# Spacing of the spectrum units, the gate of the second filter group, and one table copy in a Fourier mixing and MLP kernel

## The chip, the cores and the metric

The kernel runs on one core of one Trainium2 chip. The metric is the device time of one execution in microseconds. A core has a matrix engine (TensorE, PE in the profile; PEld is its weight load), a vector engine (VectorE, DVE), a scalar engine (ScalarE, ACT), a general engine (GpSimd, POOL) and a queue engine (SyncE, SP). DMAs are issued from SP, ACT and POOL, and 16 DMA engines carry them. Matrix results land in PSUM and are evicted from there by VectorE or ScalarE.

## The reference

```python
def _attn_ref(x, filt_r, filt_i):            # x: (8, 3008, 256)
    X = np.fft.rfft(x, axis=1)
    Y = X * (filt_r + 1j * filt_i)[None, :, :]
    return np.fft.irfft(Y, n=x.shape[1], axis=1).astype(np.float32)

def _moe_ref(x, w_in, w_out, beta):          # d_model 256, d_ff 2048
    h = x @ w_in
    g = h * (1.0 / (1.0 + np.exp(-beta * h)))
    return (g @ w_out).astype(np.float32)

out = _moe_ref(_attn_ref(x, filt_r, filt_i).reshape(24064, 256), w_in, w_out, beta)
```

Eight images of 3008 positions and 256 channels are each filtered in the frequency domain along the positions, and all 24064 rows then go through a two-layer network with a Swish whose slope is per hidden unit.

## The kernel before

**The transform.** 3008 is 47 times 64. The kernel computes the real Fourier transform by matmuls with small tables: a first stage over 47 points, with data `x` and table `t1` (`s1`, L610, line L616), a second over 64 points with `t2` (`s23`, L631, line L638), then the product with the filter, the inverse over 64 points with `t3` (line L664), and the inverse over 47 points with `t4` (`s4`, L679, its matmuls in `last4`, L541). Between the stages the data is turned through DRAM scratch: `a1` is written as `d` (L621) and read back as `a2` (L628), `z` is written as `d` (L669) and read back as `zz` (L676). All these DMAs are on SP's queue, in the order of the program, and each waits there for what it needs; the stores of the result (`store`, L784) share that queue.

**The main loop** (L812) has 47 blocks of 512 rows, each of 16 steps, 752 in all. A step has two matmuls of 128x512 into `hps` (L825), an activation by ScalarE into `gT` (L834), and, two steps later, four matmuls of 128x256 into the accumulators `acc` (L867). At the end of a block VectorE and ScalarE evict `acc` to `ost`. The transform of image b+1 is laid between these steps: `place` (L693) spreads a list of units over a range of steps, `plan` holds for each step the units in the order in which they were placed, and they are issued after the step's `hps` matmuls and before its `acc` matmuls. A first placed unit goes to the start of the range, the following ones to evenly spaced steps rounded down; with `clear` a unit is moved off the first two and last two steps of a block; a step takes at most `per` units.

**A spectrum unit** (`s23`, 15 per image) covers two of the 24 frequencies. Unit i issues two matmuls L638 into a PSUM tile `ps2`, three VectorE operations that read it and the filter (`p_t` L649, `q_t` L650 and L653), an addition `v_t` on GpSimd (L654), and, for the v of three units earlier (VLAG), two matmuls L664 into a PSUM tile `ps3`, which ScalarE evicts to `z` (L667, in the profile as L107). Units 0 to 2 have only the first half, units 12 to 14 only the second. After every third `z` the group is written as `d`. `ps2` and `ps3`, and the PSUM tiles of `s1`, `s4`, `turn_z` and `last_z`, come from one pool, `fpsum`, tag "f", of 3 buffers.

**The start** (up to L591) treats image 0 apart and through no DRAM. GpSimd issues six DMAs of `x` (X_FIRST, L124), the third of which holds j = 8 to 15 and the fifth j = 16 to 23 of 80 partitions, then the first of four groups of the filter `fri`. The other three groups (12 DMAs) are on SP behind a small DMA `mark` (L198), which reads a row of `x` and so waits for the chunk that holds it. VectorE computes angles for the first half of the table `t2`, GpSimd for the second (`angles`, L260); ScalarE turns them into sines and cosines (`t2_part`), and `t2_more` (L287) completes a half by three operations: the negated cosines, a copy of the sines (slot 2 to 3) and a copy of the cosines (slot 1 to 0). The `held` copies (L407) on GpSimd wait for the filter's third group and stand before the loads of `win_sb`, `w_out` and the first half of image 1 on GpSimd's queue. Then a loop of 14 rounds (L490 on) has `product(i)`, two VectorE multiplications by the filter (L444), transposes, tables and `inverse3` (L461).

Of the kernel before, what the change touches and what calls it, by code (L numbers as in the profile page):

```python
# [9 lines left out]
P = 128  # L10
# [3 lines left out]
F32 = mybir.dt.float32  # L14
# [10 lines left out]
M = 64  # L25
H = M // 2
NK = 24
J = 32
KG = 6
NG = NK // KG  # L30
JG = 8
# [6 lines left out]
def kernel(  # L38
# [10 lines left out]
    nc = tc.nc  # L49

    B, S, D = x.shape
# [35 lines left out]
    fri = consts.tile([P, NK, D], F32, name="fri", tag="fri")  # L87
# [6 lines left out]
    t2 = consts.tile([P, NK, 5, M], BF16, name="t2", tag="t2")  # L94
# [18 lines left out]
    def load_x(b, parts, t=None):  # L113
        if t is None:
            t = xpool.tile([NP, J, D], BF16, name="xg", tag="xg")
        xv = x[b].rearrange("(p j) d -> p j d", j=J)
        for p0, p1, j0, j1 in parts:
            nc.gpsimd.dma_start(t[p0:p1, j0:j1, :], xv[p0:p1, j0:j1, :])  # L118
        return t
# [3 lines left out]
    X_HALVES = [(0, 80, 0, J // 2), (80, NP, 0, J // 2), (0, 80, J // 2, J), (80, NP, J // 2, J)]  # L123
# [16 lines left out]
    def staged(i):  # L140
        return frr[:, NK - NFB + i * WG : NK - NFB + (i + 1) * WG, :]

    def load_wout(i):
        nc.gpsimd.dma_start(
            staged(i),
            moe_w_out[i * WG * P : (i + 1) * WG * P, :].rearrange("(fb fp) j -> fp fb j", fp=P),
        )
# [12 lines left out]
    setup = sp.enter_context(tc.tile_pool(name="setup", bufs=1))  # L160
# [32 lines left out]
    x_cur = load_x(0, X_FIRST)  # L193
# [1 line left out]
    nc.sync.dma_start(bt[:], moe_beta.rearrange("(fb fp) -> fb fp", fp=P))  # L195

    mark = dpool.tile([1, D], BF16, name="mark", tag="mark")
    nc.sync.dma_start(mark[:], x_cur[:1, JG, :])  # L198

    gp = nc.gpsimd  # L200
    ip_f = small("ip_f")
# [55 lines left out]
    NH = NK // 2  # L257
# [16 lines left out]
    def t2_part(h, part):  # L274
        u, r = us[h], rs[h]
        ks_ = slice(h * NH, (h + 1) * NH)
        if part == 0:
            nc.scalar.activation(t2[:, ks_, 2, :], u[:], ACT.Sin, scale=TWO_PI)
        elif part == 1:
            nc.scalar.activation(r[:], u[:], ACT.Abs)  # L280
        else:
            for cols, sgn, b in ((slice(0, H), -1.0, hp), (slice(H, M), 1.0, hm)):
                nc.scalar.activation(
                    t2[:, ks_, 1, cols], r[:, :, cols], ACT.Sin, scale=sgn * TWO_PI, bias=b[:]
                )

    def t2_more(h, eng):  # L287
        ks_ = slice(h * NH, (h + 1) * NH)
        nc.vector.tensor_scalar_mul(t2[:, ks_, 4, :], t2[:, ks_, 1, :], -1.0)
        eng.tensor_copy(t2[:, ks_, 3, :], t2[:, ks_, 2, :])  # L290
        eng.tensor_copy(t2[:, ks_, 0, :], t2[:, ks_, 1, :])


    m_p = small("m_p")
# [23 lines left out]
    def first1(i, on_act):  # L318
        for dc in range(NDC):
            if dc:  # L320
                ps = opsum.tile([P, 4, P], F32, name="psa", tag="acc")
            else:
                ps = fpsum.tile([P, 4, P], F32, name="psa", tag="f")
            for e in range(4):
                nc.tensor.matmul(  # L325
                    ps[:, e, :KP],
                    lhsT=x_cur[:, 4 * i + e, dc * P : (dc + 1) * P],
                    rhs=t1b[:],
                    start=True,
                    stop=True,  # L330
                )
            evac(
                a_t[:, dc, :, 4 * i : 4 * i + 4, :].rearrange("p k j a -> p j k a"),
                ps[:, :, :KP].rearrange("p j (k a) -> p j k a", a=4),
                on_act[dc],
            )
# [33 lines left out]
    first1(3, (False, False))  # L370
    warm(2)

    t2_more(0, nc.vector)
    first1(4, (False, False))
    warm(2)
    first1(5, (True, True))
# [24 lines left out]
                )  # L401
        evac(a2s[-1][:, 3 * (i % 2) : 3 * (i % 2) + 3, :], pb[:], on_act)


    held = setup.tile([P, 1], F32, name="held", tag="held")
    for p0 in (H, M + H):
        gp.tensor_copy(held[p0 : p0 + H], fri[p0 : p0 + H, 3 * KG - 1, :1])  # L407
    def load_win(h):
        fs = slice(h * FF // 2, (h + 1) * FF // 2)
        gp.dma_start(win_sb[:, :, fs], moe_w_in[:, fs].rearrange("(dc p) f -> p dc f", p=P))  # L410

    load_win(0)
    load_win(1)
    load_wout(0)
    xs = {}
    if B > 1:
        xs[1] = load_x(1, X_HALVES[:2])
    turn_a(0, False)
    turn_a(1, True)

# [59 lines left out]
    def table4():  # L480
        for src, dst in ((t1b, t4b), (t1, t4)):
            tp = opsum.tile([KP, NP], BF16, name="tp", tag="acc")
            nc.tensor.transpose(tp[:], src[:], ident[:NP, :NP])
            nc.scalar.activation(dst[:], tp[:], ACT.Copy)
# [4 lines left out]
    for i in range(NK // 2 + FLAG):  # L489
        if 0 < i < NK // 2:  # L490
            product(i)
        if i % 3 < 2 and i // 3 < 3:
            turn_a(2 + 2 * (i // 3) + i % 3, True)
        if i < 3:
            t2_part(1, i)
        if i in TAB:
            n = TAB.index(i)
            table3(1 + n // 2, 2 - 2 * (n % 2), n % 2 == 0 or n == 5)()
        if i == 3:
            t2_more(1, nc.vector)  # L500
            for h in range(1, 4):
                load_wout(h)
            if B > 1:
                load_x(1, X_HALVES[2:], xs[1])
                mark3 = dpool.tile([1, D], BF16, name="mark3", tag="mark3")
                nc.sync.dma_start(mark3[:], xs[1][:1, J - 1, :])
        if i == 11:
            table4()

            bps = hpsum.tile([P, NFB], F32, name="bps", tag="hps")  # L510
            nc.tensor.transpose(bps[:], bt[:], id_f[:])
            nc.scalar.activation(beta_sb[:], bps[:], ACT.Copy)
        if i == NK // 2:
            nc.vector.reciprocal(rbeta_sb[:], beta_sb[:])
        if i >= FLAG:
            inverse3(i - FLAG)
# [106 lines left out]
    def a2_read(b):  # L623
        s = st[b]
        s["a2"] = []
        for h in range(NG):
            t = a2pool.tile([P, KG, D], BF16, name="a2", tag="a2")
            nc.sync.dma_start(t[:], s["d1c"][:, h * KG : (h + 1) * KG, :])  # L628
            s["a2"].append(t)
# [60 lines left out]

    plan = {}

    def place(a, z, units, clear=False, per=1):  # L693
        last_at = a
        for n, go in enumerate(units):
            at = a + (z - a) * n / max(1, len(units) - 1)
            at = max(int(at), last_at)
            if clear and (at % NFB < 2 or at % NFB > 13):
                at += (2 - at) % NFB
            while len(plan.get(at, ())) >= per:  # L700
                at += 1
            plan.setdefault(at, []).append(go)
            last_at = at
        return last_at

    def u1(b, act=False):
        def unit(i):
            def go():
                if i == 0:
                    start(b)  # L710
                s1(b, i, act and i % 2 == 1)

            return go

        return [unit(i) for i in range(J // 2)]

    def u23(b):
        return [lambda i=i: s23(b, i) for i in range(NK // 2 + VLAG)]
# [4 lines left out]
    def uz(g, act=False):  # L723
        return [lambda i=i: turn_z(g, i) for i in range(2)] + [
            lambda i=i: last_z(g, i, act) for i in range(2 * NDC)
        ]
# [26 lines left out]
    units = uz(3, True)  # L753
# [4 lines left out]
    if B > 1:  # L758
        units = u1(1, True)
        place(3, 8, units[: J // 4], per=2)  # L760
        place(10, 10, uf(0, JG), per=9)
        at = place(9, 14, units[J // 4 :], per=9)
        place(at + 1, at + 1, [lambda: a2_read(1)] + uf(JG, NK), per=9)
        place(14, 20, ut(4), per=2)
        at = place(25, 56, u23(1), per=2)
        assert at < 60
        place(60, 60, [lambda: zz_read(1)], per=9)
        place(67, 79, u4(1), per=2)
    if B > 2:
        place(36, 36, ux(2), per=9)  # L770
        at = place(50, 66, u1(2, True), per=3)
        assert at < 74
        place(74, 74, [lambda: a2_read(2)], per=9)
    for b in range(2, B):
        a = first_step[b - 1]
        place(a + 3, a + 47, u23(b), True)
        place(a + 53, a + 53, [lambda b=b: zz_read(b)], per=9)
        if b + 1 < B:
            place(a + 6 if b == 2 else a - 8, NBLK * NFB, ux(b + 1), per=9)
            place(a + 48, a + 61, u1(b + 1))  # L780
            place(a + 68, a + 68, [lambda b=b: a2_read(b + 1)], per=9)
        place(a + 63, a + 78, u4(b))
# [29 lines left out]
    for s in range(len(steps) + LAG):  # L812
        if s < len(steps):
            i, fb = steps[s]
# [4 lines left out]
            while pos < t0 + tn:  # L819
                b, n0 = divmod(pos, S)  # L820
# [20 lines left out]
        if s >= LAG:  # L841
            i, fb = steps[s - LAG]
# [15 lines left out]
            per = acc[0].shape[1]  # L858
# [16 lines left out]
            if fb == NFB - 1:  # L875
                for h, a in enumerate(acc):
# [5 lines left out]
                    eng = nc.scalar if last and h >= 2 else nc.sync  # L882
# [31 lines left out]
```

## Time and profile before

| | us |
|---|---|
| median of 3 runs | 785.22 (784.85 to 785.43) |
| profiled execution | 785.37 |
| its span on the core | 783.3 |
| PE busy | 768.8 (98%) |
| PEld busy | 547.8 (70%) |
| ACT busy | 594.4 (76%) |
| DVE busy | 393.3 (50%) |
| POOL busy | 144.4 (18%) |
| HBM | 57.16 MB read, 46.66 MB written |

The granted TensorE clock is 1.0 throughout. Times in the profile count from the start of the span. In a timeline row the first number is the start, the second the duration, then engine, line, operation, output and inputs, and what the engine waited for just before. Matmuls are pipelined and their ends are modelled, so the distance between the starts of two matmuls says more than the idle time between them. Where a helper evicts PSUM, the line is the helper's (L107 for ScalarE, L109 and L111 for VectorE). A few matmul records are missing from the trace and leave a hole of the matmul's own length.

### The profile page before, as it was taken

What the parts mean: (1) busy time and instruction counts of PE and PEld (TensorE: products, weight loads), DVE (VectorE), ACT (ScalarE), POOL (GpSimd) and SP (SyncE); (2) the same over time, 40 slices, a digit from 0 to 9 for tenths busy, and PEclk for the clock granted to TensorE, in tenths of its full rate; (3) what the DMA queues carried; (4) which work ended last, traced back from release to release, by engine and by line L of the source; (5) the groups of instructions that cost most, each with busy time, mean ns of one, the idle gap of its engine ahead of it and who ended that gap; (6) DMA issues with size and microseconds to landing.
All of it is one profiled execution on the core that took longest, in us unless ns stands there. A gap on an engine that the chain in (4) does not pass through costs nothing.

```text
span 783.3 us, 15454 instructions
## 1 busy us (share of the span) xinstructions
PE 768.8 (98%) x6015; PEld 547.8 (70%) x6111; DVE 393.3 (50%) x645; ACT 594.4 (76%) x922; POOL 144.4 (18%) x143
## 2 busy tenths in 40 slices
PE   8899999999999999999999999999999999999997
PEld 5767667666776667866668666786667766776665
DVE  7848836646446563474635746267452761500101
ACT  6987887886678867787677876778767788677776
POOL 8522501320013100231002310024000330000000
PEclk9999999999999999999999999999999999999999
DMA  9979764517801186022850238412371114100101
GB/s 190 253 174 228 176 191 132 128 67 202 221 28 68 68 209 194 28 81 94 197 167 28 95 111 183 149 64 81 108 209 40 64 68 128 49 34 28 55 28 54
DMA packets 84185, 91.46 MB, mean 117 GB/s; under 512 B 4498, under 2 KB 74276, under 8 KB 83154
## 3 DMA queue, kind: packets, MB, share of 16 engines
q1 hardware_dynamic: 81008, 73.95, 30.8%
q0 software_dynamic: 2816, 16.26, 10.7%
q8 instruction: 48, 0.79, 0.4%
q10 hardware_dynamic: 288, 0.26, 0.1%
q14 instruction: 25, 0.20, 0.1%
HBM read 57.16 MB, written 46.66 MB: 133 GB/s over the span
## 4 chain that ended last, share of the span: by engine, by line
PE 96%; ACT 1%; issue 1%; DMA 1%; DVE 1%; POOL 0%; DVEq 0%; POOLq 0%
PE acc L867 43%; PE hps L825 39%; PE ps L616 3%; PE ps L541 3%; PE ps L664 3%; PE ps L638 2%; DMA xg<-in_x_dram 1%; PE psz L461 1%; PE pz L533 0%; PE psa L325 0%; ACT a L107 0%; DVE q_t L653 0%; DVE q_t L650 0%; PE pt L351 0%; PE ps L435 0%
## 5 line engine op out<-in xcount | busy, mean ns | idle before, releaser
L834 ACT ACTIVATE gT<-hps,beta_sb 128x512 bf16<-128x512 f32 x752 | 515.6, 687 | 176.5 <-PE hps L825 155.4
L867 PE MATMUL acc<-wout_sb,gT 128*128 128x256 bf16 x3008 | 451.4, 272 | 2.7
L825 PE MATMUL hps<-y,win_sb 128*128 128x512 bf16 (+8 forms) x1636 | 427.6, 350 | 0.4 <-ACT gT L834 0.3
L867 PEld LDWEIGHTS <-gT 128*128 128x128 bf16 x3008 | 285.6, 98 | 127.6 <-ACT gT L834 0.2
L825 PEld LDWEIGHTS <-win_sb 128*128 128x128 bf16 x1730 | 165.0, 98 | 24.7 <-issue 0.6
L654 POOL TENSOR_TENSOR v_t<-p_t,q_t 128x512 bf16<-128x512 f32 x84 | 106.6, 1269 | 390.4 <-DVE q_t L653 327.6
L109 DVE COPY ost<-acc 128x512 f32<-128x512 f32 (+1 forms) x88 | 56.2, 677 | 192.6 <-PE acc L867 189.6
L109 DVE CAST a<-ps 96x512 bf16<-96x512 f32 x96 | 65.9, 686 | 87.3 <-PE ps L616 86.8
L111 DVE TENSOR_SCALAR y<-ps 128x376 bf16<-128x376 f32 (+1 forms) x119 | 63.9, 544 | 61.3 <-PE ps L541 61.2
L649 DVE TENSOR_TENSOR p_t<-ps,frr 128x512 f32<-128x512 f32 x84 | 58.1, 692 | 31.3 <-PE ps L638 28.9
L653 DVE TENSOR_TENSOR q_t<-ps,fri 64x512 f32<-64x512 f32 x84 | 58.2, 693 | 1.2
L650 DVE SCALAR_TENSOR_TENSOR q_t<-ps,fri 64x512 f32<-64x512 f32 x84 | 57.4, 684 | 1.1
L541 PEld LDWEIGHTS <-zz 96*128 96x128 bf16 x512 | 35.3, 97 | 29.3 <-issue 0.5
L107 ACT ACTIVATE z<-ps 128x512 bf16<-128x512 f32 x84 | 49.5, 589 | 0.0
L616 PE MATMUL ps<-xg,t 94*96 94x512 bf16 x112 | 42.1, 381 | 0.7
L541 PE MATMUL ps<-t,zz 96*128 96x94 bf16 x448 | 36.7, 205 | 1.1
L664 PE MATMUL ps<-v_t,t 128*128 128x256 bf16 x168 | 32.2, 274 | 0.8 <-DVE q_t L653 0.3
L638 PE MATMUL ps<-a,t 128*128 128x256 bf16 x168 | 32.1, 273 | 0.4
L118 POOL DMA_DIRECT2D xg<-in_x_dram x22 | 12.1, 552 | 101.7 <-PE acc L867 97.6
L638 PEld LDWEIGHTS <-t 128*128 128x128 bf16 x168 | 15.8, 98 | 14.6
L664 PEld LDWEIGHTS <-t 128*128 128x128 bf16 x168 | 15.3, 98 | 10.8 <-ACT z L107 3.8
L616 PEld LDWEIGHTS <-t 94*96 94x96 bf16 x112 | 13.6, 123 | 11.8
(120 smaller groups left out, 195.0 us busy)
## 6 DMA issues: line engine op xcount, KB each, us to landing
out_dram<-ost SPq DMA_DIRECT2D x80, 256.0 KB, 2.1
d<-a SPq DMA_DIRECT2D x28, 384.0 KB, 3.4
a<-d SPq DMA_DIRECT2D x28, 384.0 KB, 4.4
d<-z SPq DMA_DIRECT2D x28, 384.0 KB, 2.3
zz<-d SPq DMA_DIRECT2D x28, 384.0 KB, 6.8
xg<-in_x_dram POOLq DMA_DIRECT2D x6, 1280.0 KB, 10.0
frr<-in_filt_r_dram SPq DMA_DIRECT2D x12, 256.0 KB, 7.5
out_dram<-ost SPq DMA_DIRECT2D x18, 128.0 KB, 2.5
```

What stands on the lines that cost most here:

```text
L109: nc.vector.tensor_copy(dst, src)
L111: nc.vector.tensor_scalar_mul(dst, src, scale)
L541: nc.tensor.matmul(ps[:, e, :NP], lhsT=zz[:, jj + e, dc * P : (dc + 1) * P], rhs=tab[:], start=True, stop=True,)
L616: nc.tensor.matmul(ps[:KP], lhsT=t1[:], rhs=s["x"][:, 2 * i : 2 * i + 2, :], start=True, stop=True)
L638: nc.tensor.matmul(ps[:, e, :], lhsT=t2[:, k0 + e, 3:5, :].rearrange("p c k -> p (c k)"), rhs=s["a2"][g][:, kk + e, :], start=True, stop=True,
L649: nc.vector.tensor_tensor(p_t[:], ps[:], frr[:, ks_, :], ALU.mult)
L653: nc.vector.tensor_tensor(q_t[:M], ps[M:P], fri[M:P, ks_, :], ALU.mult)
L654: nc.gpsimd.tensor_tensor(v_t[:], p_t[:], q_t[:], ALU.add)
L664: nc.tensor.matmul(ps[:, e, :], lhsT=t3[:, k0 + e, :], rhs=v_t[:, e, :], start=True, stop=True)
L825: nc.tensor.matmul(hps[:, pos - t0 : pos - t0 + ln], lhsT=win_sb[:, dc, fb * P : (fb + 1) * P], rhs=ys[b][:, dc, n0 : n0 + ln], start=(dc ...
L834: nc.scalar.activation(gT[:, :tn], hps[:, :tn], ACT.Silu, scale=beta_sb[:, fb : fb + 1])
L867: nc.tensor.matmul(acc[tb // per][:, tb % per, :], lhsT=g_[:, tb * P : (tb + 1) * P], rhs=wout_sb[:, f_, :], start=(f_ == 0 and tb % per = ...
```

## The change

1. `place` gets a parameter `gap`, the least distance in steps between consecutive units of a list. The spectrum units use 2: those of image 1 (also spread over 25 to 58 in place of 25 to 56) and those of images 2 to 7.
2. The first transform of image 2 goes to steps 54 to 68 instead of 50 to 66, and its `a2_read` to 75 instead of 74.
3. `mark` reads row j = 16 of `x` instead of j = 8, so the SP loads of filter groups 2 to 4 start behind the fifth DMA of `x` (the third chunk along j) instead of the third DMA.
4. The copy of the sines becomes `t2_sin`. For the first half it stays on VectorE; for the second it is on GpSimd, in round 0 of the loop, behind its angles. `t2_more` keeps the other two operations.
5. The `held` copies and the loads behind them become `late_loads`, called in round 0 after that copy. On GpSimd's queue their order among themselves is unchanged.

```diff
-    nc.sync.dma_start(mark[:], x_cur[:1, JG, :])
+    nc.sync.dma_start(mark[:], x_cur[:1, 2 * JG, :])
...
-    def t2_more(h, eng):
+    def t2_sin(h, eng):
+        ks_ = slice(h * NH, (h + 1) * NH)
+        eng.tensor_copy(t2[:, ks_, 3, :], t2[:, ks_, 2, :])
+
+    def t2_more(h):
         ks_ = slice(h * NH, (h + 1) * NH)
         nc.vector.tensor_scalar_mul(t2[:, ks_, 4, :], t2[:, ks_, 1, :], -1.0)
-        eng.tensor_copy(t2[:, ks_, 3, :], t2[:, ks_, 2, :])
-        eng.tensor_copy(t2[:, ks_, 0, :], t2[:, ks_, 1, :])
+        nc.vector.tensor_copy(t2[:, ks_, 0, :], t2[:, ks_, 1, :])
...
-    t2_more(0, nc.vector)
+    t2_sin(0, nc.vector)
+    t2_more(0)
...
+    def late_loads():
+        held = setup.tile([P, 1], F32, name="held", tag="held")
+        for p0 in (H, M + H):
+            gp.tensor_copy(held[p0 : p0 + H], fri[p0 : p0 + H, 3 * KG - 1, :1])
+        load_win(0)
+        load_win(1)
+        load_wout(0)
+        if B > 1:
+            xs[1] = load_x(1, X_HALVES[:2])
...
+        if i == 0:
+            t2_sin(1, gp)
+            late_loads()
...
-            t2_more(1, nc.vector)
+            t2_more(1)
...
-    def place(a, z, units, clear=False, per=1):
+    def place(a, z, units, clear=False, per=1, gap=0):
         last_at = a
         for n, go in enumerate(units):
             at = a + (z - a) * n / max(1, len(units) - 1)
-            at = max(int(at), last_at)
+            at = max(int(at), last_at + gap if n else last_at)
...
-        at = place(25, 56, u23(1), per=2)
+        at = place(25, 58, u23(1), per=2, gap=2)
...
-        at = place(50, 66, u1(2, True), per=3)
-        assert at < 74
-        place(74, 74, [lambda: a2_read(2)], per=9)
+        at = place(54, 68, u1(2, True), per=3)
+        assert at < 75
+        place(75, 75, [lambda: a2_read(2)], per=9)
     for b in range(2, B):
         a = first_step[b - 1]
-        place(a + 3, a + 47, u23(b), True)
+        place(a + 3, a + 47, u23(b), True, gap=2)
```

More of the change, by code (lines that the diff above doesn't have):

```diff
@@ L402, in turn_a @@
         evac(a2s[-1][:, 3 * (i % 2) : 3 * (i % 2) + 3, :], pb[:], on_act)
-    held = setup.tile([P, 1], F32, name="held", tag="held")
-    for p0 in (H, M + H):
-        gp.tensor_copy(held[p0 : p0 + H], fri[p0 : p0 + H, 3 * KG - 1, :1])
     def load_win(h):
@@ L410, in load_win @@
         gp.dma_start(win_sb[:, :, fs], moe_w_in[:, fs].rearrange("(dc p) f -> p dc f", p=P))
-    load_win(0)
-    load_win(1)
-    load_wout(0)
     xs = {}
-    if B > 1:
-        xs[1] = load_x(1, X_HALVES[:2])
+    def late_loads():
[7 more added lines that the diff above has]
+            xs[1] = load_x(1, X_HALVES[:2])
     turn_a(0, False)
```

## The prediction

> **What bounds the kernel now.** I first read the chain of work that ended last on the page, then busy time by stage:
>
> ```profile
> PE 96%; ACT 1%; issue 1%; DMA 1%; DVE 1%; POOL 0%; DVEq 0%; POOLq 0%
> ```
>
> ```profile
> 0.00:36.00 36.00, 31.88 (x377) 24.16 (x380) 30.77 (x81) 27.50 (x52) 25.69 (x44) 1.00 0.97 211
> 95.00:783.30 688.30, 679.51 (x5191) 483.28 (x5274) 321.92 (x502) 519.29 (x790) 97.51 (x83) 1.00 0.36 104
> ```
>
> (Stage, length, then busy us of PE, PEld, DVE, ACT, POOL, the clock, the DMA share, GB/s.) From 95 us on TensorE is busy 679.51 of 688.30 us; ACT has 25% to spare, DVE half. Only idle TensorE can be won there. In the first 36 us three engines are close together and the DMA is full (0.97). Part of the remaining 8.8 us is no idleness: matmul records are missing in places, a hole of one 128x512 matmul (0.217 us) each. So I read waits, where the weight load in front of a stalled matmul shows them best (line, releaser: us, times, longest):
>
> ```profile
> PEld L664 <- ACT z L107: 3.8, 12, 0.5
> ...
> PEld L664 <- DVE q_t L653: 1.2, 2, 0.6
> ```
>
> Twelve waits of L664, the spectrum unit's second pair of matmuls, on ACT's eviction of z. One of them, with the unit before and the unit after:
>
> ```profile
> 159.97 0.38 PE L638 MATMUL ps<-a,t 128*128 128x256 bf16 x2
> 160.19 0.38 PE L664 MATMUL ps<-v_t,t 128*128 128x256 bf16 x2
> ...
> 161.06 0.38 PE L638 MATMUL ps<-a,t 128*128 128x256 bf16 x2
> 161.46 0.39 PE L664 MATMUL ps<-v_t,t 128*128 128x256 bf16 x2
> ...
> 163.64 0.38 PE L638 MATMUL ps<-a,t 128*128 128x256 bf16 x2
> 163.86 0.38 PE L664 MATMUL ps<-v_t,t 128*128 128x256 bf16 x2
> ```
>
> L638 to L664 takes 0.22 us in the first and third unit, 0.40 in the second, so its stall is 0.40 - 0.22 = 0.18 us (0.186 unrounded). The second is one step behind the first (1.09 us). All three "f" PSUM buffers are then taken: two by ps2 tiles that VectorE still reads (0.69 + 0.68 + 0.69 = 2.07 us a unit, rows of L649, L650, L653), one by the z that ACT evicts. The third unit is two steps behind the second and waits for nothing.
>
> The start has another bound; its chain (start, us, what):
>
> ```profile
> 21.99 0.71 ACT a L107
> 22.75 0.61 PE psz L461 x8
> ...
> 31.26 0.06 PE tp L483 x2
> 31.32 0.68 DVE qb_t L444
> ...
> 32.05 0.23 PE bps L511
> ```
>
> ACT carries it from 16.83 to 22.7, TensorE to 31.3, then VectorE's product for 0.7 us. The filter wait in front of VectorE's first product (0.86 us, ended at 16.67) is not on this chain.
>
> **What the Trainium skill says.** "Perfetto Trace Analysis", section Identifying Performance Opportunities: the same gap repeating on the engine that should be saturated can mean too few SBUF or PSUM buffers. The trace agrees: 12 equal waits on three buffers. "DMA: Bandwidth & Descriptors", section Queues, rings and completion order: each DMA engine goes round robin between queues that have work, a packet at a time. The trace disagrees at this place: SP issues filter loads from 9.44 us, yet the queue table of 9 to 13 us shows
>
> ```profile
> q0 software_dynamic: 274, 0.99, 104.2%
> q1 hardware_dynamic: 2, 0.00, 0.1%
> ```
>
> so SP's queue (q1) moved nothing before GpSimd's (q0) was nearly drained. "GPSIMD Engine Reference", section Engine selection, calls one-input work on GpSimd roughly line rate; no large copy on POOL is in the trace. "SBUF — State Buffer", section SBUF: two separate sides: a GpSimd operation and a VectorE operation with two SBUF inputs or in a two-port mode exclude each other. The products read one PSUM operand; they stay at 0.68 us while POOL computes (16.7 to 18.3 us).
>
> **The change, part by part.**
>
> *Units two apart, images 2 to 7.* Working through `place` by hand: units 5, 6, 10 and 11 move from steps a+19, +21, +35, +37 to +20, +22, +36, +38; nothing else in these images moves. Exactly the pairs one step apart disappear, 2 in each of 6 images, the 12 waits. Stall by stall (distance L638 to L664 less 0.22): 0.38 for the first (144.6 us), 0.186 for eleven: 0.38 + 11 x 0.186 = 2.43 us. At +20 the z of +18 has long been evicted (ACT ended it at 161.40; the new L664 would come at about 162.4). VectorE has 2 x 0.87 (159.54 - 158.67, a step without a unit) + 0.43 = 2.17 us from one unit to the next against 2.07 of work, as between +19 and +21 now. The next units (+25, +40) are still 3 and 2 steps away. The d and zz transfers keep their steps, for unit 14 does not move. Bounds: 0 (each wait returns in another form) to -2.43; I take -2.4.
>
> *Image 1.* Units go from 25..56 to 25..58, the x transform of image 2 from 50..66 to 54..68. Now L664 at 84.58 loses 0.65 - 0.22 = 0.43 us and L541 at 75.34 about 0.43 (one matmul record is missing there), both behind VectorE; another at 93.9 loses 0.07. In step 42 a filter unit and a `last_z` share three buffers; unit 8 moves to 43, so 0.43 goes, and 0.07 with it, since products no longer meet the x transform. But unit 4 joins `last_z` at step 34 while VectorE, backlogged by y evictions since 65.7 us, still ends unit 3 only at 75.3. Third allocation of that step: about 74.9, so 0.3 to 0.65 us of waiting takes the place of 0.43. Step 50 repeats this pattern without backlog. Sum: -0.4, bounds -0.9 to +0.3. What becomes later: the last d write by two steps (2.1 us). The semaphore of the first zz read is full 4.66 us after its issue at 104.36, at 109.0; 2.1 later is 111.1, and L541 wants it at 112.5. The read of a2 moves one step, but SP only gets there at 120.09 and the first use is at 129.5. Both hidden, with 1.4 and several us.
>
> *The sines' copy.* VectorE loses the first of these two:
>
> ```profile
> 22.33 0.34 DVE L290 COPY t<-t 128x768 bf16<-128x768 bf16 x1
> 22.59 0.57 DVE L291 COPY t<-t 128x768 bf16<-128x768 bf16 x1
> ```
>
> Start to start that is 22.59 - 22.33 = 0.26 us. VectorE is unbroken from here to the qb_t on the chain, so 0.26 arrives there; TensorE is ready at 31.35, so up to 0.70 would count. On POOL the copy waits for ACT's sines (end 18.37). Its price there is not shown: 0.6 us scaled from POOL's 94x96 copy (0.25 us against 0.18 for one element), 1.5 to 1.8 us at the two-input rows of 768 elements. I take 0.9: it ends at 19.3, while POOL anyway idles 1.72 us until the filter lands at 19.9. At 1.8 it ends at 20.2 and still precedes the second `held` copy (21.20), which sets when win is issued (21.44). Its readers (product 6, about 24.3; table 2 parts) come later. Free at both ends; bare, 3 us more would delay win by 2.
>
> *The gate.* Chunk 5, which holds step 16 of x, lands 7.5 us after its issue at 3.70: 11.2 instead of 9.1 for chunk 3. The mark and 12 filter DMAs on SP start 2.1 us later; behind them SP has nothing until 44.6. As q1 got no bytes before 13 anyway, and each issue (0.47 us) is faster than its transfer (about 0.8), I expect its data 0 to 0.5 us later. Landings of group 1: about 16.8 to 19.0 (the issue slots that SP gets back tell them), needed at 20.73. Gain: group 0's last packets no longer share an engine with q1, VectorE starts 0 to 0.4 earlier (ps2 is ready at 16.2, and ACT's tables at 21.51 cap it at 0.4). Loss: if q1 starts the full 2 us late, group 1 lands at 21, product 3 stalls 0.4, and win, w_out and x of image 1 come 2 us late; of these x's second half, landing at 45.2 for its use at 47.1, is tight. Bounds -0.4 to +1.0; I take -0.1.
>
> Sum: -2.4 - 0.4 - 0.26 - 0.1 = -3.2 us. The profiled execution took 785.37 us (span 783.3 plus 2.1 around it), the median of the runs is 785.22: I take -3.2 from the median, 782.0 us.
>
> **The rivals.**
>
> *The gate opens a hole.* q1 starts 2 us late and the DMA idles: +1.0 in place of -0.1. For it: the mark itself took 3.4 us from issue to bytes. Against: q0 is full to 14 us, and `bt` on an idle queue took 1.4 us to land. Total -2.1: 783.1 us.
>
> *The waits only move.* With other buffers rotating, the L664 behind each moved unit waits for VectorE instead of ACT, and nothing is won in images 2 to 7: 785.2 - 0.8 = 784.4. Against: the +21 and +37 units, two steps behind their forerunners, run at 0.22.
>
> *Slower.* Same place, full price: each of the 24 moved units waits as L664 at 84.58 did, for the previous unit's ps2 (0.43): 24 x 0.43 = 10.3, less 3.2, is 792.3 us. It decides from (3.2 + 1.6) / 24 = 0.20 us per unit. It needs all of the 0.1 us margin (2.17 against 2.07) to be gone and more.
>
> **How the numbers follow.** No change means within 0.2%, 1.6 us, about what a measurement here can tell. Forecast as worked out 0.66 (781.0 to 783.2); hole 0.17 (782.6 to 783.9); waits only move 0.11 (783.8 to 785.4); slower 0.06. Faster (under 783.65) gets 0.66 + 0.15 + 0.01, within 0.2% gets 0.12, slower 0.06. The range leaves out the slow case, most of the third and a little below the first: 780.9 to 784.0.
>
> **What the profile after would show.** The twelve L664 waits on z gone, L638 to L664 0.22 everywhere after 130 us; about 3.2 us less span. L290's row on POOL under 1.8 us, before `held`; VectorE with two table operations near 22. The mark at 11.2, and the win issue no later than 22. A wait at step 34 (about 75 us) on q_t remains. Wrong would be: L664 waits on DVE behind the moved units, a product waiting for filter after 20 us, hps or ps waiting for win or xg before 48 us.

## The result and the profile after

| | before | after |
|---|---|---|
| median of 6 runs, us | 785.04 (784.70 to 785.71) | 782.70 (782.23 to 783.21) |
| profiled execution, us | 785.37 | 782.91 |
| its span, us | 783.3 | 780.9 |

The changed kernel takes 0.9969 of the time before, 95% interval [0.9956, 0.9982]: 2.34 us less, where 3.2 were worked out. In the lines of the changed kernel the transform's second stage is L648 (before L638), its inverse L674 (L664), the filter product L659, L660 and L663 (L649, L650, L653), the inverse over 47 points L551 (L541), the first stage L626 (L616), the start's product L451 (L444), the main loop L835, L844 and L877.

The chain of work that ended last, of the changed kernel, and its busy time by stage (stage, length, then PE, PEld, DVE, ACT, POOL, the clock, the DMA share, GB/s):

```profile
PE 95%; DVE 2%; ACT 1%; issue 1%; DVEq 0%
```

```profile
0.00:36.00 36.00, 32.97 (x383) 24.73 (x384) 30.91 (x82) 27.84 (x54) 26.58 (x45) 1.00 0.98 205
95.00:780.90 685.90, 681.92 (x5274) 484.12 (x5272) 322.71 (x503) 519.22 (x790) 98.01 (x83) 1.00 0.36 105
```

From 95 us the span is shorter by 688.3 - 685.9 = 2.4 us, as much as the whole span. So all that was gained in the net lies there, and what changed ahead of 95 us cancels out. The weight loads' waits of the changed kernel show the same (line, releaser: us, times, longest):

```profile
PEld L187 <- issue: 3.3, 12, 0.3
PEld L674 <- DVE q_t L663: 1.8, 3, 1.0
```

The twelve waits on ACT's z are gone. The waits on q_t were 1.2 us in two places and are 1.8 in three, the longest 1.0 instead of 0.6. TensorE's timeline of the changed kernel, at the units that the prediction showed:

```profile
159.68 0.38 PE L648 MATMUL ps<-a,t 128*128 128x256 bf16 x2
159.90 0.38 PE L674 MATMUL ps<-v_t,t 128*128 128x256 bf16 x2
161.85 0.38 PE L648 MATMUL ps<-a,t 128*128 128x256 bf16 x2
162.07 0.38 PE L674 MATMUL ps<-v_t,t 128*128 128x256 bf16 x2
```

Two steps apart (2.17 us), every unit goes through at 0.22 us.

At the start, GpSimd's timeline of the changed kernel has the copy where it was to be:

```profile
18.43 0.82 POOL L289 COPY t<-t 128x768 bf16<-128x768 bf16 x1
20.88 0.18 POOL L418 COPY held<-fri 32x1 f32<-32x1 f32 x1 [1.63 <-DMA fri<-in_filt_r_dram]
```

The copy takes 0.82 us, and behind it GpSimd still idles 1.63 us for the filter. The win load is issued at 21.88 us (the prediction's limit was 22), VectorE has two table operations left (21.54 and 21.81), the mark is issued at 10.95 us, and the queue table of 9 to 13 us has one queue alone:

```profile
q0 software_dynamic: 261, 0.94, 104.3%
```

The start's chain of the changed kernel (start, us, what):

```profile
31.54 0.23 PE bps L521
```

This is 0.51 us earlier than before (32.05). It looks like the predicted 0.36 and more; the experiments show that it isn't the change's doing.

### The profile page after: what moved, and what is told of

It reads as the page before. It is cut to its first block, busy times and chain, and to the rows that moved or that the text cites. A ratio compares the mean times of both kernels' runs of the same rounds, so it can differ in the third digit from the quotient of the medians.

```text
span 780.9 us, 15549 instructions
## 1 busy us (share of the span) xinstructions
PE 772.5 (99%) x6111; PEld 549.0 (70%) x6111; DVE 392.8 (50%) x644; ACT 594.3 (76%) x922; POOL 145.3 (19%) x144
## 4 chain that ended last, share of the span: by engine, by line
PE 95%; DVE 2%; ACT 1%; issue 1%; DVEq 0%
PE acc L877 42%; PE hps L835 41%; PE ps L626 3%; PE ps L551 3%; PE ps L674 2%; PE ps L648 2%; PE pw L187 1%; DVE qb_t L451 0%; DVE a_t L109 0%; ACT a L107 0%; DVE q_t L660 0%; PE pz L543 0%; DVE q_t L663 0%; DVE p_t L659 0%; ACT z_t L107 0%
## 5 line engine op out<-in xcount | busy, mean ns | idle before, releaser
L844 ACT ACTIVATE gT<-hps,beta_sb 128x512 bf16<-128x512 f32 x752 | 515.4, 687 | 174.0 <-PE hps L835 163.3
L877 PE MATMUL acc<-wout_sb,gT 128*128 128x256 bf16 x3008 | 451.4, 272 | 0.0
L835 PE MATMUL hps<-y,win_sb 128*128 128x512 bf16 (+8 forms) x1730 | 447.8, 351 | 0.3 <-ACT gT L844 0.3
L877 PEld LDWEIGHTS <-gT 128*128 128x128 bf16 x3008 | 285.7, 98 | 128.1 <-ACT gT L844 0.2
L835 PEld LDWEIGHTS <-win_sb 128*128 128x128 bf16 x1730 | 164.9, 98 | 24.7 <-issue 0.6
L664 POOL TENSOR_TENSOR v_t<-p_t,q_t 128x512 bf16<-128x512 f32 x84 | 106.7, 1270 | 387.7 <-DVE q_t L663 377.6
L659 DVE TENSOR_TENSOR p_t<-ps,frr 128x512 f32<-128x512 f32 x84 | 58.1, 691 | 29.9 <-PE ps L648 28.0
L663 DVE TENSOR_TENSOR q_t<-ps,fri 64x512 f32<-64x512 f32 x84 | 58.3, 694 | 1.2
L660 DVE SCALAR_TENSOR_TENSOR q_t<-ps,fri 64x512 f32<-64x512 f32 x84 | 57.5, 684 | 1.1
L551 PEld LDWEIGHTS <-zz 96*128 96x128 bf16 x512 | 35.3, 97 | 28.9
L626 PE MATMUL ps<-xg,t 94*96 94x512 bf16 x112 | 41.9, 381 | 0.1
L551 PE MATMUL ps<-t,zz 96*128 96x94 bf16 x448 | 36.7, 204 | 0.0
L674 PE MATMUL ps<-v_t,t 128*128 128x256 bf16 x168 | 32.1, 273 | 1.0 <-DVE q_t L663 1.0
L648 PE MATMUL ps<-a,t 128*128 128x256 bf16 x168 | 32.1, 273 | 0.0
L648 PEld LDWEIGHTS <-t 128*128 128x128 bf16 x168 | 15.8, 98 | 14.4
L626 PEld LDWEIGHTS <-t 94*96 94x96 bf16 x112 | 13.6, 123 | 11.9
L674 PEld LDWEIGHTS <-t 128*128 128x128 bf16 x168 | 16.1, 98 | 7.8 <-DVE q_t L663 1.8
```

What stands on the lines that cost most here:

```text
L551: nc.tensor.matmul(ps[:, e, :NP], lhsT=zz[:, jj + e, dc * P : (dc + 1) * P], rhs=tab[:], start=True, stop=True,)
L626: nc.tensor.matmul(ps[:KP], lhsT=t1[:], rhs=s["x"][:, 2 * i : 2 * i + 2, :], start=True, stop=True)
L648: nc.tensor.matmul(ps[:, e, :], lhsT=t2[:, k0 + e, 3:5, :].rearrange("p c k -> p (c k)"), rhs=s["a2"][g][:, kk + e, :], start=True, stop=True,
L659: nc.vector.tensor_tensor(p_t[:], ps[:], frr[:, ks_, :], ALU.mult)
L663: nc.vector.tensor_tensor(q_t[:M], ps[M:P], fri[M:P, ks_, :], ALU.mult)
L664: nc.gpsimd.tensor_tensor(v_t[:], p_t[:], q_t[:], ALU.add)
```

## The experiments

The theory after the result: images 2 to 7 give some -2.4, image 1 costs something instead of giving 0.4, and the start gives between 0 and -0.5. The rival: everything gave what was worked out, and 0.9 was lost in another place. Each part was run alone, and image 1 was undone in the changed kernel. Every run's difference is taken to the kernel before, measured beside it on the same chip.

### Images 2 to 7 alone

```diff
-    def place(a, z, units, clear=False, per=1):
+    def place(a, z, units, clear=False, per=1, gap=0):
...
-            at = max(int(at), last_at)
+            at = max(int(at), last_at + gap if n else last_at)
...
-        place(a + 3, a + 47, u23(b), True)
+        place(a + 3, a + 47, u23(b), True, gap=2)
```

> The kernel before with the distance of two steps for the spectrum units of images 2 to 7 alone. Theory (the twelve waits of the second matmul pair on the eviction of z go, and nothing comes in their place): 2.43 us off the kernel before, ratio 0.9969, no such wait after 130 us. Rival (the waits only move, and the gain of the whole change comes from the start): within 0.5 us of the kernel before, with the waits on VectorE in their place.

Measured: 782.57 us (782.38 to 783.45) beside 785.19 of before on the same chip, ratio 0.9969 [0.9958, 0.9980], so -2.6 us. All twelve waits on z are gone, and those ahead of 115 us are what they were. This part alone gives as much as the whole change: the rest of it sums to about nothing, within the width of these intervals (some 0.9 us to either side).

### Image 1 alone

```diff
-        at = place(25, 56, u23(1), per=2)
+        at = place(25, 58, u23(1), per=2, gap=2)
...
-        at = place(50, 66, u1(2, True), per=3)
-        assert at < 74
-        place(74, 74, [lambda: a2_read(2)], per=9)
+        at = place(54, 68, u1(2, True), per=3)
+        assert at < 75
+        place(75, 75, [lambda: a2_read(2)], per=9)
```

> The kernel before with image 1's new schedule alone (units over 25 to 58, transform of image 2 in 54 to 68, its read at 75). Theory now (the move of unit 4 behind the eviction of the second block puts VectorE behind a store, and stalls follow): 0.4 to 0.8 us slower than before, with VectorE idle about 1.4 us ahead of the ost copy near 76 us and matmul waits near 74, 84 and 112 us. The prediction's view: 0.4 us faster.

Measured: 785.78 us (784.61 to 786.28, 13 runs), ratio 1.0004 [0.9996, 1.0013]: +0.6 us by the medians and +0.3 by the ratio, with an interval of -0.3 to +1.0 that just leaves out the predicted -0.4. Its runs lie apart: two at 784.6 and 784.7 us, one of them the profiled one, the other eleven between 785.4 and 786.3. The reason is read from the changed kernel's trace.

### Where image 1 loses

TensorE's timeline at unit 8, which the change moves from step 42 to 43 to be rid of 0.43 us, of the kernel before, then of the changed kernel:

```profile
83.93 0.38 PE L638 MATMUL ps<-a,t 128*128 128x256 bf16 x2
84.58 0.39 PE L664 MATMUL ps<-v_t,t 128*128 128x256 bf16 x2 [0.26 <-DVE q_t L653]
```

```profile
84.47 0.38 PE L648 MATMUL ps<-a,t 128*128 128x256 bf16 x2
85.56 0.39 PE L674 MATMUL ps<-v_t,t 128*128 128x256 bf16 x2 [0.71 <-DVE q_t L663]
```

L648 to L674 takes 1.09 us in the changed kernel, a stall of 1.09 - 0.22 = 0.87. VectorE is late, and its timeline of the changed kernel says since when:

```profile
76.31 0.69 DVE L109 COPY ost<-acc 128x512 f32<-128x512 f32 x1 [1.44 <-DMA out_dram<-ost]
77.03 0.69 DVE L659 TENSOR_TENSOR p_t<-ps,frr 128x512 f32<-128x512 f32 x1
```

and the same piece of before:

```profile
75.32 0.69 DVE L649 TENSOR_TENSOR p_t<-ps,frr 128x512 f32<-128x512 f32 x1
...
77.45 0.69 DVE L109 COPY ost<-acc 128x512 f32<-128x512 f32 x1
```

At the end of step 33 VectorE evicts half of the second block to an `ost` buffer, which is free only when the two stores of half of the first block are complete. Before, unit 4 stood in step 33, ahead of this copy in VectorE's queue; its three operations filled the time and the copy waited for nothing. With the gap unit 4 stands in step 34, behind the copy. VectorE idles 1.44 us in front of it, with unit 4's p_t queued behind: 77.03 instead of 75.32. The queue is backlogged, so this delay runs on to unit 8. Why the store is late stands on SP's queue, in its timeline of the changed kernel:

```profile
65.44 0.31 SPq L134 DMA_DIRECT2D frr<-in_filt_r_dram  x1
66.75 5.55 SPq L810 DMA_DIRECT2D out_dram<-ost  x4
```

The two stores that hold the buffer are the first of this row, behind eight filter loads of 256 KB. They are issued at 66.75 and 69.17 and, by the trace's records of their ends, complete at 75.88 and 76.19, 9.1 and 7.0 us later; the copy starts at 76.31. Between 300 and 700 us a store of before lands in 2.1 us (median).

Two further kernels test this. The first undoes image 1 alone in the changed kernel; the second is the changed kernel once more.

```diff
-        at = place(25, 58, u23(1), per=2, gap=2)
+        at = place(25, 56, u23(1), per=2)
...
-        at = place(54, 68, u1(2, True), per=3)
-        assert at < 75
-        place(75, 75, [lambda: a2_read(2)], per=9)
+        at = place(50, 66, u1(2, True), per=3)
+        assert at < 74
+        place(74, 74, [lambda: a2_read(2)], per=9)
```

> The changed kernel with image 1's schedule of before. Theory: faster than the changed kernel by 0.4 to 0.8 us, so 2.9 to 3.2 us off the kernel before, ratio 0.996. The prediction's view of image 1: 0.4 us slower than the changed kernel, so 2.0 us off the kernel before.

Measured: 782.38 us (782.25 to 782.85), ratio 0.9963 [0.9950, 0.9975]. That is 0.3 under the changed kernel by the medians. By the differences to the kernel before (-2.8 here, -2.34 for the changed kernel and -2.45 for its second run below), image 1 costs 0.4 to 0.5. The sign agrees with image 1 alone, but a cost of this size is well inside the intervals (-2.8 stands for anything from -3.9 to -2.0), so the times alone don't show it.

> The changed kernel once more, for comparison on one chip with the next two: 2.4 us off the kernel before. Theory: near 76 us VectorE again idles ahead of the second block's ost copy (0.3 to 1.5 us, by how late the first stores land), and the matmul wait of unit 8 near 84.6 us is the longer the longer this was. Rival (the waits near 74 and 84 us come from the new steps alone): the same waits, whatever that idle time is.

Measured: 782.44 us (782.07 to 783.30), ratio 0.9972 [0.9960, 0.9983]. In this execution VectorE's copy waited only 0.46 us:

```profile
75.73 0.69 DVE L109 COPY ost<-acc 128x512 f32<-128x512 f32 x1 [0.46 <-PE ps L674]
```

and the stall at step 43 was 0.08 us instead of 0.87. The row names TensorE's L674, but the wait was again for the store. The second of the two stores was complete at 75.60, and the copy starts 0.13 us later; in image 1 alone (waited 0.31 us) these were 74.99 and 75.11, in the first run 76.19 and 76.31. With four buffers (below) the same copy starts at 75.50, before the L674 of its step:

```profile
75.53 0.39 PE L674 MATMUL ps<-v_t,t 128*128 128x256 bf16 x2 [0.32 <-DVE q_t L663]
```

In all three executions this second store is issued (67.70, 68.30 and 69.17) within 0.02 us of the end of the second of the eight filter loads (67.68, 68.28, 69.16) and is complete 7.0 to 7.3 us later. In these three executions, the later that load landed, the longer the copy waited, and where the copy waited 0.31 and 0.46 us, unit 8 stalled for 0.08 us, where it waited 1.44, for 0.87. So the price of the misplaced unit depends on when the stores are through, and differs between executions of the same kernel.

What image 1's schedule is worth can be read free of the start. Where two kernels do the same work, their profiles agree closely if they are counted from the first activation of the main loop (the rows of `gT`) and not from the start of the span. At step 80 nothing of image 1's new schedule is left, and the first spectrum unit of image 2 stands at step 83. From the activations of the first step and of step 80 in each profile, us:

| profile | first to step 80 | step 80 to the end |
|---|---|---|
| before | 90.09 | 656.31 |
| images 2 to 7 alone | 90.09 | 653.80 |
| image 1 undone in the changed kernel | 90.09 | 653.78 |
| start alone | 90.09 | 656.34 |
| image 1 alone | 89.79 | 656.34 |
| changed kernel, second run | 89.80 | 653.78 |
| changed kernel | 90.70 | 653.78 |

Images 2 to 7 are worth 656.31 - 653.78 = 2.53 us in either run of the changed kernel. Image 1's schedule gains 0.29 us in the two executions in which the store comes early, and costs 0.61 in the one in which it comes late (0.10 of it arises before step 16, ahead of every moved unit).

Next, two cures: a fourth `ost` buffer (its room taken from `a2pool`), and unit 4 put back ahead of the copy.

```diff
-    a2pool = pool("a2pool", 5)
+    a2pool = pool("a2pool", 4)
...
-    ostp = pool("ostp", 3)
+    ostp = pool("ostp", 4)
```

> The changed kernel with four ost buffers instead of three (and four a2 buffers instead of five, to make room). Theory: VectorE no longer waits for a store near 76 us, so unit 4's products start at about 75.6 instead of 77.0, the wait of unit 8 near 84.6 us (0.88) falls under 0.1, and the time is 0.4 to 0.9 us under the changed kernel. Rival (the steps alone): no change beyond 0.2 us, the wait at 84.6 stays.

```diff
-        at = place(25, 58, u23(1), per=2, gap=2)
+        for n, go in enumerate(u23(1)):
+            s_ = max(int(25 + 33 * n / 14), 0) - (n in (3, 4))
+            at = place(s_, s_, [go], per=2)
```

> The changed kernel with units 3 and 4 of image 1 at their steps of before (31 and 33), so that unit 4's VectorE work stands ahead of the second block's ost copy again; all else as changed. Theory: no idle VectorE near 76 us, the wait near 84.6 us gone, and last_z near 75 us waits 0.43 again in place of L674's 0.47: 0.5 to 0.9 us under the changed kernel, 3 us off the kernel before. Rival (the x transform of image 2 in later steps is what costs): no gain, as the wait of 0.28 near 112 us is all that matters.

Measured: with four buffers 782.34 us (782.08 to 782.96), ratio 0.9969 [0.9956, 0.9981]; with unit 4 back at step 33 (and unit 3 at 31) 782.08 us (781.99 to 782.66), ratio 0.9966 [0.9953, 0.9978]. The copy in VectorE's timeline, with four buffers, then with the unit moved back:

```profile
75.50 0.69 DVE L109 COPY ost<-acc 128x512 f32<-128x512 f32 x1
```

```profile
77.07 0.69 DVE L109 COPY ost<-acc 128x512 f32<-128x512 f32 x1
```

Neither waits any more, and in both no weight load of L674 waits at step 43 (0.18 us is left there, in front of L551). The mechanism is shown. Its size in the times is small: 0.1 and 0.36 us under the changed kernel's second run, less than was expected of either and inside the intervals. The profiles agree: from the first activation to step 80 these two take 89.89 and 89.81 us, about as much as the second run (89.80), which had hardly paid the wait, and 0.8 to 0.9 less than the first run (90.70), which had paid it.

The last of image 1 keeps unit 4 back, evicts image 0's group 2 with ScalarE in turn instead of VectorE alone, and starts the first transform of image 2 at step 52:

```diff
-    place(15, 29, uz(2))
+    place(15, 29, uz(2, True))
...
-        at = place(54, 68, u1(2, True), per=3)
+        at = place(52, 66, u1(2, True), per=3)
```

> The changed kernel with units 3 and 4 of image 1 at steps 31 and 33, the third z group of image 0 evicted by ScalarE instead of VectorE, and the x transform of image 2 in steps 52 to 66. Theory (image 1's waits come from VectorE's backlog and from three PSUM tiles in one step): the waits near 74 (0.43), 83 (0.18) and 111 us (0.28) fall to under 0.1 each, so 0.7 to 0.9 us under the one with units 3 and 4 moved alone, 3.5 us off the kernel before. Rival (ScalarE, at 76%, becomes late in steps 20 to 30): new waits of hps on gT there, no gain.

Measured: 782.08 us (781.67 to 782.36), ratio 0.9960 [0.9947, 0.9972], 3.0 us under the 785.10 of before beside it. All waits of its weight loads between 60 and 130 us, where the changed kernel has the 1.8 us of L674:

```profile
PEld L551 <- issue: 0.3, 1, 0.3
PEld L674 <- DVE q_t L663: 0.2, 1, 0.2
```

A backlogged VectorE was what image 1 waited for; with some of its work on ScalarE the wait at 74 us is gone, and with the transform two steps earlier that at 112 us (below). This is the best version of all. Its lead over the changed kernel, 0.4 to 0.7 us by medians or by differences to before, is inside the intervals; in its profile it reaches step 80 in 89.20 us, 0.6 less than the second run of the changed kernel.

### The start

```diff
-        at = place(25, 58, u23(1), per=2, gap=2)
+        at = place(25, 56, u23(1), per=2)
...
-        place(a + 3, a + 47, u23(b), True, gap=2)
+        place(a + 3, a + 47, u23(b), True)
```

(the changed kernel with images 1 to 7, and the transform and `a2_read` of image 2, as before: only the start is new)

> The kernel before with the later gate and the sines' copy on GpSimd alone, all steps of the main loop as before. Theory: 0.5 us off (the first hps matmul at 35.75 instead of 36.26 us), ratio 0.9993, and nothing of it given back later. Rival (x of image 1, which lands 1.4 us later, is waited for): 0 or slower, with a wait of the first transform on xg near 47 us.

Measured: 784.78 us (784.60 to 786.16, 13 runs), ratio 0.9996 [0.9988, 1.0004]. Then its two parts, each in the kernel before: the gate (`mark` reads `2 * JG`), and the sines' copy with `late_loads`.

> The kernel before with the mark moved to the third chunk alone. Theory now (the start's end is set by TensorE and by how much one DMA engine lags in the execution at hand, not by the gate): within 0.15 us of the kernel before where both have the lag or both have not; the filter's group 1 lands no more than 0.5 us later. The prediction's view: 0.1 us faster. Rival (a hole in the DMA): up to 1 us slower, with no bytes of the SP queue before 15 us.

> The kernel before with the sines' copy of the table's second half on GpSimd alone. Theory now (TensorE holds the pace from product 5 on, so what VectorE saves is idle again there): VectorE's table work 0.26 us shorter, a wait of product 5 on TensorE near 23.6 us in its place, the first hps matmul no more than 0.1 us earlier than in a kernel before with the same lag of the DMA; 0 to 0.2 us in the time. The prediction's view: 0.26 us.

Measured: gate 784.96 us (784.59 to 785.37, 13 runs) beside 784.89, ratio 0.9999 [0.9991, 1.0008]; sines 784.87 us (784.58 to 785.25, 13 runs) beside 785.10, ratio 0.9995 [0.9987, 1.0003]. No part of the start can be told from nothing.

The first activation of the main loop in each profile tells where the 0.51 us comes from. It starts at 36.89 in before and at 36.38 in the changed kernel; but it also starts at 36.41 and 36.40 in the kernels that keep the old start (images 2 to 7 alone, image 1 alone), and at 36.85 in the second run of the changed kernel. What goes with it is the landing of the first x loads. The median of the first four (the last number, us), in the DMA table of the kernel before, then of image 1 alone:

```profile
xg<-in_x_dram POOLq DMA_DIRECT2D x4, 320.0 KB, 7.0
```

```profile
xg<-in_x_dram POOLq DMA_DIRECT2D x4, 320.0 KB, 5.8
```

Where it is 7.0 to 7.6 us, the main loop starts between 36.81 and 37.15 (seven profiles, old and new start), where it is 5.8 to 6.5, between 36.38 and 36.51 (six, old and new): about half a microsecond that comes and goes with the execution. The two profiles compared at first were a late one and an early one. Within a group the new start is no earlier: 36.38 to 36.51 against 36.40 and 36.41, and 36.82 to 37.15 against 36.89.

And the 0.26 us that VectorE saves? Its timeline with the new start alone, whose x landed in 5.9 us:

```profile
23.62 0.69 DVE L451 TENSOR_TENSOR pb_t<-ps,fri 128x512 bf16<-128x512 f32 x1 [0.24 <-PE ps L442]
...
30.82 0.68 DVE L451 TENSOR_TENSOR qb_t<-ps2q,fri 128x512 bf16<-128x512 f32 x1
```

and with image 1 alone, the old start (5.8 us):

```profile
23.65 0.68 DVE L444 TENSOR_TENSOR pb_t<-ps,fri 128x512 bf16<-128x512 f32 x1
...
30.83 0.68 DVE L444 TENSOR_TENSOR qb_t<-ps2q,fri 128x512 bf16<-128x512 f32 x1
```

The operation before these begins at 22.69 with the new start, 0.36 us earlier than at 23.05 with the old; then VectorE waits 0.24 us for TensorE's L442, and the one on the chain is at 30.82 against 30.83. VectorE's saving became a wait of VectorE. The second run of the changed kernel, whose x landed late, has the same wait of 0.24 us (at 24.07).

### When a unit one step behind another costs

To see whether every close pair costs, five pairs per image in place of two, in the kernel before:

```diff
-        place(a + 3, a + 47, u23(b), True)
+        at_ = (3, 4, 9, 12, 13, 19, 20, 25, 26, 34, 35, 37, 40, 43, 50)
+        for n, go in enumerate(u23(b)):
+            place(a + at_[n], a + at_[n], [go])
```

> The kernel before with its spectrum units of images 2 to 7 moved so that each image has four neighbouring pairs with both ps2 and ps3 (steps +12/+13, +19/+20, +25/+26, +34/+35) instead of two, and one pair without ps3 (+3/+4). Theory (the cost is the second L664 waiting for the first one's z in the one free PSUM buffer): 24 waits of about 0.19 us instead of 12, 2.2 us slower than before, none at +4. Rival (neighbouring units cost as such, by VectorE's backlog): waits on VectorE, at +4 too, and more than 3 us.

Measured: 783.52 us (783.35 to 784.33, 16 runs), ratio 0.9981 [0.9973, 0.9988]: 1.6 us faster than before (1.35 from step 80 to the end of its profile), where both theories had it slower. Its weight loads' waits:

```profile
PEld L664 <- ACT z L107: 1.8, 6, 0.3
```

Six, one per image, all at +35, and none at the four other pairs. TensorE's timeline of this kernel at +25 and +26:

```profile
150.61 0.38 PE L664 MATMUL ps<-v_t,t 128*128 128x256 bf16 x2
...
151.91 0.38 PE L664 MATMUL ps<-v_t,t 128*128 128x256 bf16 x2
```

and at +34 and +35:

```profile
159.29 0.38 PE L664 MATMUL ps<-v_t,t 128*128 128x256 bf16 x2
...
160.16 0.38 PE L638 MATMUL ps<-a,t 128*128 128x256 bf16 x2
160.57 0.39 PE L664 MATMUL ps<-v_t,t 128*128 128x256 bf16 x2
```

ACT's timeline ends the z of the first pair 151.23 + 0.59 - 150.61 = 1.21 us after its L664 started, and that of the second 159.92 + 0.59 - 159.29 = 1.22. At +25 a step is 1.30 us from one L664 to the next (four matmuls into acc between, from 150.82), so z is out. At +34 the step is the third of a block, where the first hidden group's acc matmuls are halved (two from 159.51; the other two go to the step after): the next L664 could come at 160.16 + 0.22, 1.09 us behind the first, and waits to 1.28. Both costly pairs of before, +18/+19 and +34/+35, are of this kind; of the pairs tried, no other cost anything.

## Why the prediction was nearly right, step by step

**Images 2 to 7: right.** The twelve stalls (one of 0.38 us and eleven of 0.19, so not all equal) summed to 2.43, I took -2.4, the part alone measured -2.6, and the profiles give -2.53 from step 80 on. The named cause (an f buffer held by z) was right; "one step behind" was too wide, since among the pairs tried it costs only in the third and fourth step of a block. For this change that made no difference: all twelve were such pairs.

**Image 1: the step that failed.** Predicted -0.4 (bounds -0.9 to +0.3). The profiles give -0.29 in two executions and +0.61 in one; the times lean to the costly side (+0.6 alone by the medians, +0.4 to +0.5 by undoing it), with wide intervals. The wait at step 34 came as worked out (0.48 us at 74.93, in the bounds of 0.3 to 0.65). The failure is the sentence that unit 8 moves to step 43, "so 0.43 goes". It looked at who shares the buffers in step 43 and not at what unit 4 is put behind: the `ost` copy at the end of step 33, which waits for a store. Where the store is early, the 0.43 does go (0.08 is left); where it is late, 0.87 takes its place.

Two more sizes were wrong, and that they nearly cancel is luck. A new stall of 0.28 us at 112 us was missed: two L551 groups and an L626 share the three f buffers in step 67, into which the later transform of image 2 now reaches. And "another at 93.9 loses 0.07" is a misreading. The lines of before:

```profile
93.68 0.59 PE L825 MATMUL hps<-y,win_sb 128*128 128x512 bf16 x2
94.40 0.39 PE L664 MATMUL ps<-v_t,t 128*128 128x256 bf16 x2
94.68 0.38 PE L616 MATMUL ps<-xg,t 94*96 94x512 bf16 x1
```

Two matmuls of 0.217 us end at 94.11, so L664 is 0.29 us late, and L616 behind it 0.28 - 0.22 = 0.06. The prediction's 0.07 is what is left if 0.22 of this is taken for a missing record, but the row has both matmuls of its step (x2), and the gate alone stalls there for the same 0.29. So the stalls of image 1 in before are 0.43 + 0.43 + 0.29 + 0.06 = 1.21. In the changed kernel's profile they are 0.48 + 0.87 + 0.28 + 0.07 = 1.70, in its second run 0.48 + 0.08 + 0.28 + 0.07 = 0.91. The differences, +0.49 and -0.30, are what the counts to step 80 show (+0.61, of which 0.10 arises before step 16, and -0.29).

**The sines' copy: operation right, gain wrong.** 0.82 us on GpSimd against 0.9, hidden by 1.63 us of idleness. (The scaling from the 94x96 copy, with the 0.18 us of one element kept, is 0.18 + 8 x 0.07 = 0.74 and not 0.6.) But the 0.26 was carried to the chain because VectorE was "unbroken from here to the qb_t on the chain". It was unbroken only as it had just enough to do: L442 on TensorE was the next limit, 0.24 us away. It is worth nothing measurable.

**The gate: right on the queue.** SP's loads had moved nothing before 13 us, and delaying their issue by 1.8 us (11.26 instead of 9.44) cost nothing; -0.1 was taken, the gate alone gives +0.1 with an interval of about 0.7 to either side.

The sum by the profiles: -2.53, image 1 between -0.29 and +0.61, and 0 for the start are -2.8 to -1.9; the change gave -2.34, and -2.45 in its second run. In the two profiles compared at first an early start (-0.51) happened to cover a late store (+0.61), so that the span's -2.4 is by chance what images 2 to 7 gave alone.

**The rivals.** The hole didn't open: GpSimd's queue alone kept the DMA at 104.3% of 16 engines from 9 to 13 us, and the product at 20.34 us did not wait for the filter. In images 2 to 7 the waits didn't move to VectorE. The slower rival's picture, an L674 waiting for the previous unit's q_t, did appear, but at a unit of image 1 and at none of the 24 moved units of images 2 to 7, and at twice the price (0.87). The prediction named it as a sign of being wrong; its cause was the store and not the margin of 2.17 against 2.07 us.

## What to carry to other kernels

Before moving work by one step, list what stands between its old and its new place on every engine's queue that it uses: here one copy that waits for a store, which the moved work had covered. A busy engine without gaps is a bound only if its inputs are early; look how long ago each was ready before a saving on it is carried to the end. Before a difference of half a microsecond between two single profiles is put down to a change, look whether executions of one kernel differ by as much, and count the stages from an event inside the kernel: here parts that differed by 0.5 us from the start of the span agreed within 0.03 us from the first activation. A hole that looks like a missing record is one only if the record is missing: count the matmuls of the row.

## What was not expected of the hardware

- The first x loads land in 5.8 to 7.6 us (median of four) from execution to execution of kernels that issue them alike, and the main loop starts about 0.45 us later where they land late. In the kernel before, 15 of the 16 parts of the third x load were down at 7.64 us and the last at 9.11; in image 1 alone all 16 were down at 7.50.
- Stores issued behind eight filter loads on SP's queue were complete 7.0 to 9.1 us after their issue, against 2.1 us from issue to landing later in the kernel, and the second of them was issued in three executions only when a filter load had landed, within 0.02 us.
- GpSimd copied 128x768 bf16 from SBUF to SBUF in 0.82 us, VectorE in 0.34 to 0.57 (the rows L290 and L291 of before).
